# Batch 0's tables on GpSimd's queue, two weight pieces between the thirds of x, and E's rows copied whole

## The chip, the cores and the metric

The kernel runs on one core of one Trainium2 chip. The metric is the device time in microseconds of one execution. Times below are written in us; engines are TensorE (PE in the profile, its weight loads PEld), VectorE (DVE), ScalarE (ACT), GpSimd (POOL) and SyncE (SP), whose queue issues most transfers. Each engine runs its own instructions in the order in which they were issued to it and waits at an instruction until the semaphores that it names have been reached.

## What is computed

```python
X = np.fft.fft(x, axis=1)              # x: (8, 3008, 256) float32
X = np.fft.fft(X, axis=2).real         # Fourier mixing over sequence and features
x = X.reshape(8 * 3008, 256)
gate = 1.0 / (1.0 + np.exp(-(x @ w_gate)))   # w_gate, w_val: (256, 1536) float64
val = x @ w_val
out = gate * val @ w_out                     # w_out: (1536, 256) float64
```

The three weights are given as float64 and are turned into float32 on the chip.

## The kernel before

**The main part.** A batch is mixed in two steps: sums over the sequence with cosine and sine tables give pk and qk (`half`, `places`), and the feature transform is merged into the gate and value weights once, G = dtab x weights (`merge`, line 346, and `merged`, line 353), so that one multiplication of pk and qk with G gives gate and value (`front_a`, line 731, and `front_b`, line 742). The term of the first feature, the row E, is added through ScalarE: `seed` (line 722) writes E's chunk, spread over the partitions in EK, times the vector ge into the accumulator. The loop over `count` steps (8 batches x chunks of 252 positions x 12 tiles of d_ff) then runs front_a, gate_a, part, seed, gate_b, back and front_b, with other work hung on single steps in the dictionaries `mid`, `pre`, `use`, `side`.

**The prologue**, which the change touches, stands before that loop, from `busy = ...` on. Everything is written out by hand in order.

- *Weights* come in 18 pieces of 512 KB: 0 to 11 of gate and value in turn, 12 to 17 of w_out. `weight_load(j)` (line 257) issues the transfer on SP. `weight_parts(j)` (line 303) takes Abs of the high words and a scaled copy of the low words on ScalarE. `weight_join(j)` (line 313) does three VectorE operations through a PSUM bank (lines 322, 323, 325) and an integer add on GpSimd (line 327). `piece(j)` is four matmuls of the joined piece with dt into a bank `ps`; `merged(j)` copies that bank to G on ScalarE (line 358); `ge_load(j)` (line 371) sends two rows of G back through SP as two columns each of ge.
- *x of batch 0* comes in three thirds of 1 MB (`load_third`, line 151, line 155), and its cosine and sine tables in six transfers of 371 KB (`load_table`, line 204, line 206), two for each third. `fold_ops(0, 2)` gives, per third, `third` (lines 498, 499, 460 on VectorE, then a small ScalarE copy of one feature to `XV`, line 516) and `feats` with `turned` (lines 505, 507, 508 on VectorE, line 510 on ScalarE). After `third` and `feats` of a third, `e0_sums(j)` adds its part to row E in bank pe, and `halves` add its part to three of the four halves of pk and qk: (block 0, pk), (block 1, pk), (block 0, qk). Half of these sums read x folded, the other half the turned copies that ScalarE makes. The fourth half, (block 1, qk), runs in one go behind the third third. Each half is then copied (line 578) and placed (lines 584, 588).
- *Row E*: `e0_heads` builds the first 252 values on VectorE (lines 644 to 646), `e0_copies` copies the four rows of bank pe on ScalarE (line 626), `e0_spread` spreads the heads over the partitions with one matmul of one row (ek), and `e0_row` places the whole row on GpSimd at step 4 of the loop.

Transfers use eight semaphores for SP's and ScalarE's queues in turn; a transfer also waits for the one issued eight before it. SP's order is: weights 0 to 3, third 0, two tables, third 1, two tables, third 2, two tables, weights 4 and 5, ge of pieces 0 to 3, weights 6 to 12, and then 14 to 17 with 13 among them, and the rest of ge.

PSUM has eight banks: three (8 - NB) rotate under the tag x, five (NB) have tags of their own, po0 to po4.

Of the kernel before, what the change touches and what calls it, by code (L numbers as in the profile page):

```python
# [53 lines left out]
NQ = 6  # L54
# [28 lines left out]
def kernel(  # L83
# [44 lines left out]
    sp = ctx.enter_context(tc.tile_pool(name="sp", bufs=2))  # L128
    cp = ctx.enter_context(tc.tile_pool(name="cp", bufs=2))
    op = ctx.enter_context(tc.tile_pool(name="op", bufs=1))  # L130
    psx = ctx.enter_context(tc.tile_pool(name="psx", bufs=8 - NB, space=PSUM))
    pso = ctx.enter_context(tc.tile_pool(name="pso", bufs=1, space=PSUM))

    def mm(o, l, r, start, stop):
        nc.tensor.matmul(o, l, r, start=start, stop=stop, skip_group_check=True)  # L135

    def bank(name, other=None):
        if other is not None:
            return pso.tile([P, 512], F32, name=name, tag=f"po{other}")
        return psx.tile([P, 512], F32, name=name, tag="x")  # L140


    X = {}
# [42 lines left out]
    HK = -(-(HE + HO) // 16) * 16  # L186
    n = 2 * NQ * HK
    ST = [st[:, 0:n].rearrange("p (t q k) -> p t q k", t=2, q=NQ)]
    XV = st[0:NP, n : n + 2 * NQ * (HD + 1)].rearrange("p (i q d) -> p i q d", i=2, q=NQ)
    assert NE == HE + HO and NO == 2 * HO and n + 2 * NQ * (HD + 1) <= LONG  # L190
    sgn = const.tile([P, 2], F32, name="sgn")
    wf = const.tile([P, NG, len(PLACE), P], F32, name="wf")
    G = const.tile([P, 2, 2, F], F32, name="G")
# [9 lines left out]

    def load_table(t, j):
        q = slice(2 * j, 2 * j + 2)
        nc.sync.dma_start(out=ST[0][0:NP, t, q, 0 : HE + HO], in_=stab[:, t, q, HO : NE + HO])

    def table_again():

# [225 lines left out]
    def sign(q, r=False):  # L435

        i = (q // 2 % 2) ^ (r and q % 2 == 0)
        return sgn[0:NP, i : i + 1]

    def fold_ops(b, nq):  # L440
# [52 lines left out]
        else:  # L493
# [14 lines left out]
                tt(lo, lo, hi, op=ALU.add)  # L508
            def turned(q):
                copy = lambda to, of, s: nc.scalar.activation(to, of, AF.Copy, scale=s)  # L510
                copy(XV[:, :, q, 0:HD], x4[:, 1::-1, q, 0:HD], sign(q.start))
                for i in range(q.start, q.stop):
                    copy(x4[:, 3:1:-1, i, HD:D], x4[:, 3:1:-1, i, 0:HD], sign(i, True))
            XR_[0] = [(XV[:, i], x4[:, 3 - i, :, HD:D]) for i in range(2)]
            for q in qs:
                ops += [lambda q=q: (third(q), nc.scalar.activation(
                            XV[:, :, q, HD], x4[:, 1::-1, q, HD], AF.Copy, scale=sign(q.start))),
                        lambda q=q: (feats(q), turned(q))]
        for blk, (v, r) in enumerate(parts):
            if b and blk:  # L520
# [8 lines left out]
    def table_of(t, q, blk, turned=False):  # L529

        if not turned:
            return ST[0][0:NP, t, q, blk * HE : HE + blk * HO]
        to = ST[0][0:NP, t ^ (q % 2), q]
        return to[:, HE + HO - 1 : HE - 1 : -1] if blk else to[:, HE - 1 : 0 : -1]

    def columns(blk):

        return (slice(HO, NE), slice(0, HO)) if not blk else (slice(0, HO), slice(HO, NO))

    def half(b, w, d, blk, sn, other=None):  # L540
# [2 lines left out]
        c0, n = ((0, NE), (NE, 2 * NJ if b else NO))[blk]  # L543
        ev, od = [bank(name, other and other[i])[:, 0:n] for i, name in enumerate(("ev", "od"))]

        def sums(*qs):
            for q in sorted(qs, key=lambda q: q % 2):
                mm((ev, od)[q % 2][:, columns(blk)[0]], w(q), table_of(int(sn), q, blk), q < 2, q >= NQ - 2)
            for q in sorted(qs, key=lambda q: q % 2):
                mm((ev, od)[q % 2][:, columns(blk)[1]], XR_[0][blk][int(sn)][:, q, 0:HD],  # L550
                   table_of(int(sn), q, blk, True), False, q >= NQ - 2)

# [29 lines left out]
    def places(d, blk, sn, ev, od, high=None, e=nc.vector):  # L582
        if not high:
            e.tensor_tensor(d[:, blk : blk + 2 * ev.shape[1] - 1 : 2], ev, od, op=ALU.add)
        if high in (None, 1):
            lo, hi = (od, ev) if sn else (ev, od)
            top = M - blk
            e.tensor_tensor(d[:, top : top - 2 * NO + 1 : -2], lo[:, 0:NO], hi[:, 0:NO],
                                    op=ALU.subtract)
# [14 lines left out]

    E0 = {}

    def e0_sums(j):

        if not j:
            E0["ps"] = bank("pe", NB - 1)  # L610
        for q in (2 * j, 2 * j + 1):
            for blk in range(2):
                row = (2 * blk + q % 2) * TB
                mm(E0["ps"][row : row + 1, columns(blk)[0]], W[0, blk][2][:, q], table_of(0, q, blk), not j, j == N3 - 1)
        for q in (2 * j, 2 * j + 1):
            for blk in range(2):
                row = (2 * blk + q % 2) * TB
                mm(E0["ps"][row : row + 1, columns(blk)[1]], XV[:, blk, q, HD : HD + 1],
                   table_of(0, q, blk, True), False, j == N3 - 1)

    def e0_copies():

        ps = E0["ps"]
        E0["v"][3] = evp.tile([P, 2 * NJ], F32, name="a", tag="a")[0:1, 0:NO]
        for i, a in enumerate(E0["v"]):
            nc.scalar.copy(a, ps[i * TB : i * TB + 1, 0 : a.shape[1]])

    def e0_row():

        er = shared["er"]  # L630
        ev, od, ev1, od1 = E0["v"]
        nc.gpsimd.memset(er[:, NK:], 0.0)
        places(er, 0, True, od, ev, e=nc.gpsimd)
        places(er, 1, False, ev1, od1, e=nc.gpsimd)

    def e0_heads():

        n = CH // 2
        full = op.tile([P, NK + 1], F32, name="er", tag="os")
        a = E0["v"] = [full[0:1, i * NE : i * NE + n] for i, n in enumerate((NE, NE, NO))]  # L640
        a.append(evp.tile([P, 2 * NJ], F32, name="a", tag="a")[0:1, 0:NO])
        h = E0["h"] = ekp.tile([P, CH], F32, name="eh", tag="ek")[0:1]
        for i in (1, 2, 3):
            nc.vector.tensor_copy(a[i][:, 0:n], E0["ps"][i * TB : i * TB + 1, 0:n])
        nc.vector.tensor_tensor(h[:, 0::2], a[1][:, 0:n], E0["ps"][0:1, 0:n], op=ALU.add)
        nc.vector.tensor_tensor(h[:, 1::2], a[2][:, 0:n], a[3][:, 0:n], op=ALU.add)

    def e0_spread(other):

        ps = bank("ek", other)[:, 0:CH]  # L650
        mm(ps, busy[0:1, 0:P], E0["h"], True, True)
        EK[0] = ekp.tile([P, CH], F32, name="ek", tag="ek")
        nc.scalar.copy(EK[0], ps)

# [289 lines left out]
    nc.gpsimd.memset(nil, 0.0)  # L944
    nc.scalar.activation(table, nil[:, 0, 0:1], AF.Sigmoid)
    nc.gpsimd.dma_start(out=zero, in_=nil)
    nc.scalar.dma_start(out=dt, in_=dtab.rearrange("(c p) d -> p c d", p=P))
    load_x(0)
    for j in range(4):
        weight_load(j)  # L950
    for j in range(N3):
        load_third(j)
        for t in range(2):
            load_table(t, j)
    for j in (4, 5):
        weight_load(j)

    def warm(n):

        ps = bank("warm", 3)  # L960
        for _ in range(n):
            mm(ps[:, 0:CH], busy[:, 0:P], busy, True, True)
# [3 lines left out]

    shared["er"] = pqp.tile([P, NK + 1], F32, name="er", tag="pk")[0:1]
    signs()
    warm(12)
    for j in range(4):  # L970
        weight_parts(j)
        weight_join(j, j % 3)
        piece(j, (None, None, None, 3)[j])
        if j > 1:
            merged(j - 2)
    merged(2)
    for j in range(3):
        ge_load(j)
    seq_start(0)
    folds = fold_ops(0, 2)  # L980
    halves = [seq_group(0, blk, 0, (2 * blk, 2 * blk + 1)) for blk in range(2)]
    halves.append(seq_group(0, 0, 1))
    for j in range(N3):
        folds[2 * j]()
        e0_sums(j)
        if not j:
            merged(3)
            ge_load(3)
            for i in (6, 7, 8, 9, 10, 11, 12):
                weight_load(i)  # L990
        folds[2 * j + 1]()
        if j == 1:
            weight_parts(4)
        for sums, _, _ in halves:
            sums(2 * j, 2 * j + 1)
    e0_heads()
    weight_join(4)
    halves[0][1]()()
    weight_parts(5)
    weight_join(5)  # L1000
    halves[1][1]()()
    halves[2][1]()()
    halves = [seq_group(0, 1, 1, (0, 1))]
    halves[0][0](*range(NQ))
    weight_parts(6)
    e0_copies()
    weight_join(6, NB - 1)
    weight_parts(7)
    weight_join(7, NB - 1)
    halves[0][1]()()  # L1010
    e0_spread(2)
    weight_parts(8)
    weight_join(8, NB - 1)
    for j in (4, 5, 6):
        piece(j)
    merged(4)
    seed(0)
    weight_parts(9)
    weight_join(9, NB - 1)
    merged(5)  # L1020
    seed(1)
    front_a(0)
    merged(6)
    seed(2)
    piece(7, 1)
    front_a(1)
    weight_parts(10)
    weight_join(10, NB - 1)
    part(0)
    part(1)  # L1030
    for i in (14, 15):
# [17 lines left out]
    def using(j):  # L1049
        weight_use(j, j % 2)  # L1050
        if jobs[j][0] < 2:
            merged(j)
    for j, i in ((11, 1), (12, 3), (13, 5), (14, 6), (15, 8), (16, 10), (17, 12)):
        if j > 10:
            pre.setdefault(i - 1, []).append(lambda j=j: weight_parts(j))
        mid.setdefault(i, []).append(lambda j=j: weight_join(j, 2))
        if jobs[j][0] == 2:
            use.setdefault(i + 2, []).append(lambda j=j: using(j))
# [138 lines left out]
```

## Time and profile before

| | us |
|---|---|
| three runs: median (least, most) | 1924.33 (1923.66, 1926.11) |
| the profiled execution, its own time | 1925.47 |
| its span, first to last instruction | 1923.7 |
| TensorE busy, share of the span | 1912.1, 99% |
| granted TensorE clock | 1.00 |

The span is the stretch that the profile shows; the time of the execution is 1.77 us longer. A timeline row reads: start, duration, engine, line, operation, output<-input, shape, count, and in brackets the idle time before it and what ended it. A float32 matmul leaves two records. Matmul records overlap, so that TensorE's busy share is no measure of its peak; where their starts are spaced evenly the engine is full. The windows view of the first 60 us, busy time of each engine (and number of instructions) in stretches of 10 us:

```profile
core 0: us, PE busy (x) PEld busy (x) DVE busy (x) ACT busy (x) POOL busy (x), PEclk, DMA share, GB/s
0.00:10.00 10.00, 7.93 (x27) 6.49 (x28) 4.75 (x10) 5.19 (x8) 2.74 (x8) 1.00 0.83 292
10.00:20.00 10.00, 8.20 (x48) 5.60 (x47) 9.12 (x17) 3.82 (x8) 4.80 (x3) 1.00 1.06 315
20.00:30.00 10.00, 9.68 (x72) 7.83 (x72) 7.79 (x13) 3.65 (x8) 0.00 (x0) 1.00 0.93 277
30.00:40.00 10.00, 8.81 (x57) 7.98 (x58) 8.04 (x18) 8.13 (x18) 2.60 (x2) 1.00 0.72 256
40.00:50.00 10.00, 10.00 (x46) 8.30 (x45) 9.40 (x16) 9.78 (x21) 4.21 (x4) 1.00 1.02 377
50.00:60.00 10.00, 8.89 (x41) 7.52 (x40) 6.78 (x13) 7.43 (x17) 3.54 (x3) 1.00 0.04 1
```

### The profile page before, as it was taken

The page shows a single profiled execution, that of the slowest core. Times are in us where ns is not written, and L with a number is a line of the kernel's source. Part 1 is how long each engine was busy: PE and PEld are TensorE (multiplying, and loading weights), DVE is VectorE, ACT ScalarE, POOL GpSimd, SP SyncE. Part 2 cuts the span into 40 slices and gives each one's busy share as a digit, 9 for nine tenths or more (in the row PEclk, how much of TensorE's full clock was granted, in tenths as well). Part 3 has the DMA queues.
Part 4 walks back from the last instruction along what each step waited for, and adds up shares of the span by engine and source line. Part 5 has one row for each costly group of instructions (what it writes and reads, how often), then busy time and mean ns, then how long its engine had stood idle before and what let it go on. Part 6 is the DMA issues. An engine that isn't in the chain of part 4 may idle for free.

```text
span 1923.7 us, 34664 instructions
## 1 busy us (share of the span) xinstructions
PE 1912.1 (99%) x11340; PEld 1793.4 (93%) x11340; DVE 1410.9 (73%) x3220; ACT 1346.3 (70%) x3158; POOL 1554.7 (81%) x2807
## 2 busy tenths in 40 slices
PE   8999999999999999999999999999999999999999
PEld 7899999999999999999999999999999999999998
DVE  7757876787767776777777777777777777766776
ACT  5877767767777677776777767777677766777775
POOL 2589989978898688986888878988788886777775
PEclk9999999999999999999999999999999999999999
DMA  9251421111020201202111020111200100000001
GB/s 305 84 91 37 106 80 57 51 62 33 20 77 26 80 18 36 68 15 80 25 48 49 20 81 21 47 51 24 80 14 15 26 16 15 15 22 20 26 17 30
DMA packets 169215, 95.62 MB, mean 50 GB/s; under 512 B 129658, under 2 KB 159940, under 8 KB 167244
## 3 DMA queue, kind: packets, MB, share of 16 engines
q1 hardware_dynamic: 168482, 92.90, 17.0%
q8 instruction: 91, 1.49, 0.3%
q14 instruction: 88, 0.72, 0.1%
q10 hardware_dynamic: 522, 0.50, 0.1%
q0 software_dynamic: 32, 0.00, 0.0%
HBM read 68.13 MB, written 47.24 MB: 60 GB/s over the span
## 4 chain that ended last, share of the span: by engine, by line
PE 96%; ACT 1%; POOL 0%; DVE 0%; issue 0%; ACTq 0%; POOLq 0%
PE pf L135 50%; PE po L135 41%; PE ev L135 2%; PE rows L135 1%; PE od L135 1%; PE row L135 0%; POOL sf L777 0%; ACT pf L729 0%; ACT G L358 0%; ACT ae L740 0%; PE pe L135 0%; ACT wf L311 0%; ACT wc L311 0%; PE ps L135 0%; POOL st L231 0%
## 5 line engine op out<-in xcount | busy, mean ns | idle before, releaser
L777 POOL TENSOR_TENSOR sf<-h 128x168 f32<-128x168 f32 (+1 forms) x935 | 516.7, 571 | 229.8 <-DVE h L771 229.2
L777 POOL TENSOR_TENSOR sf<-h,sf 128x168 f32<-128x168 f32 (+1 forms) x1122 | 614.0, 568 | 49.4 <-DVE h L771 47.9
L135 PE MATMUL pf<-qk,G 128*128 128x252 f32 (+1 forms) x2304 | 582.0, 375 | 1.3 <-ACT ae L740 1.3
L135 PE MATMUL pf<-pk,G 128*128 128x252 f32 (+1 forms) x2304 | 582.5, 376 | 0.0
L729 ACT ACTIVATE pf<-ek,ge 128x252 f32<-128x252 f32 (+1 forms) x1152 | 542.6, 471 | 19.3 <-DVE h L771 0.3
L771 DVE TENSOR_TENSOR h<-pf,z 128x252 f32<-128x252 f32 (+1 forms) x576 | 241.6, 419 | 415.2 <-ACT pf L768 413.6
L135 PE MATMUL po<-sf,wf 128*128 128x168 f32 (+1 forms) x2992 | 516.9, 306 | 0.3 <-POOL sf L777 0.2
L740 ACT ACTIVATE ae<-pf 128x504 f32<-128x504 f32 (+1 forms) x576 | 339.2, 589 | 249.2 <-PE pf L135 248.0
L135 PEld LDWEIGHTS pf<-pk,G 128*128 128x128 f32 x2304 | 437.0, 190 | 51.7 <-issue 2.0
L135 PEld LDWEIGHTS po<-sf,wf 128*128 128x128 f32 x2992 | 460.6, 190 | 9.2 <-POOL sf L777 1.0
L135 PE MATMUL po<-h,wf 128*128 128x168 f32 (+1 forms) x2618 | 463.3, 305 | 0.0
L135 PEld LDWEIGHTS pf<-qk,G 128*128 128x128 f32 x2304 | 410.8, 190 | 27.9 <-ACT ae L740 2.1
L755 DVE TENSOR_TENSOR z<-ae,pf 128x504 f32<-128x504 f32 (+1 forms) x576 | 386.0, 670 | 63.1 <-ACT h L754 58.3
L135 PEld LDWEIGHTS po<-h,wf 128*128 128x128 f32 x2618 | 416.6, 190 | 16.2
L895 DVE TENSOR_TENSOR c<-c 128x168 f32<-128x168 f32 (+1 forms) x929 | 423.5, 464 | 3.4
L754 ACT ACTIVATE h<-pf 128x252 f32<-128x252 f32 (+1 forms) x576 | 218.5, 379 | 208.5 <-PE pf L135 199.8
L767 DVE TENSOR_TENSOR h<-h,pf 128x252 f32<-128x252 f32 (+1 forms) x576 | 233.5, 405 | 0.0
L768 ACT ACTIVATE pf<-z 128x252 f32<-128x252 f32 (+1 forms) x576 | 211.4, 367 | 23.4 <-DVE h L767 20.1
L777 POOL TENSOR_TENSOR sf<-sf 128x168 f32<-128x168 f32 (+1 forms) x187 | 104.2, 557 | 14.7
L777 POOL TENSOR_TENSOR sf<-sf,h 128x168 f32<-128x168 f32 (+1 forms) x187 | 110.3, 590 | 0.0
L808 ACT COPY c<-po 128x504 f32<-128x504 f32 (+1 forms) x141 | 80.0, 568 | 0.0
L904 DVE STREAM_TRANSPOSE os<-c 128x256 f32<-128x256 f32 x184 | 79.9, 435 | 0.0
(168 smaller groups left out, 921.9 us busy)
## 6 DMA issues: line engine op xcount, KB each, us to landing
x<-xr SPq DMA_DIRECT2D x14, 1536.0 KB
out_dram<-os SPq DMA_DIRECT2D x368, 56.0 KB
xr<-in_xf_dram SPq DMA_DIRECT2D x14, 768.0 KB
xr<-in_xf_dram SPq DMA_DIRECT2D x35, 256.0 KB
ek<-ed SPq DMA_DIRECT2D x39, 126.0 KB
out_dram<-os SPq DMA_DIRECT2D x284, 7.0 KB
x<-in_xf_dram SPq DMA_DIRECT2D x3, 1024.0 KB
st<-in_stab_dram SPq DMA_DIRECT2D x4, 564.8 KB
```

The lines of the kernel that those rows point to most:

```text
L135: nc.tensor.matmul(o, l, r, start=start, stop=stop, skip_group_check=True)
L729: nc.scalar.activation(PF[i][:, g], EK[i // NFT], AF.Copy, scale=ge[:, g, f : f + 1])
L740: nc.scalar.activation(AP[i], PF[i], AF.Copy, scale=2.0)
L754: nc.scalar.activation(H[p][:, fh, 0:n], PF[i][:, 0], AF.Sigmoid)
L755: nc.vector.tensor_tensor(z[:, :, ::-1], AP.pop(i), PF[i], op=ALU.subtract)
L767: nc.vector.tensor_tensor(h[:, fh, 0:n], h[:, fh, 0:n], pf[:, 1], op=ALU.mult)
L768: nc.scalar.activation(pf[:, 0], z[:, 0], AF.Sigmoid)
L771: nc.vector.tensor_tensor(h[:, fh, n:], pf[:, 0], z[:, 1], op=ALU.mult)
L777: nc.gpsimd.tensor_tensor(block(p, dst), block(p, a), block(p, b), op=(ALU.subtract, ALU.add)[op])
L808: (nc.vector.tensor_copy if t == 1 or t == 3 and not last else nc.scalar.copy)(C[0][:, 3 * t * R : 3 * (t + 1) * R], PO[t][:, 0 : 3 * R])
L895: engine.tensor_tensor(t[:, dst * R : (dst + 1) * R], *v, op=(ALU.subtract, ALU.add)[op])
L904: nc.vector.transpose(os_[0][:, s, 0:nb, h, :], t[:, c0 : c0 + nb * TB])
```

## The change

1. **Queues.** dt moves from ScalarE's queue to SP's, behind weights 0 and 1. The six table transfers move from SP to GpSimd: the first two behind a one-element copy that waits for dt and ahead of the adds of joins 0 to 3, the other four behind those adds. SP issues weights 0, 1, dt, weights 2, 3, the three thirds, weights 4 to 7, then ge of pieces 0 to 3, weights 8 to 12.
2. **Order of ScalarE.** `merged` of pieces 0 to 2 comes after all four pairs of parts.
3. **Pieces 4 and 5.** Piece 4's parts follow third 0's turned rows on ScalarE, its join comes on VectorE between thirds 1 and 2, its matmuls between the sums of thirds 1 and 2; piece 5's parts follow third 1's turned rows, its join comes behind third 2. Joins 6 to 10 and the banks of all joins and pieces are set anew. Within a third, the sums that read x folded come before those that read turned rows. Join 11 moves from step 1 of the loop to step 2.
4. **Row E.** One ScalarE copy takes all of bank pe (128 x 377); four transfers on SP bring its four rows to partition 0; the spread is two matmuls of 126 columns with a 0/1 matrix `pair`, built with four memsets on GpSimd. Bank pe is cleared by a VectorE memset first. `e0_heads` and the three other copies go. The one turned feature lies in a tile of its own, `xe`.
5. The three rotating banks get tags x0 to x2, which the prologue can name.

```diff
-        nc.sync.dma_start(out=ST[0][0:NP, t, q, 0 : HE + HO], in_=stab[:, t, q, HO : NE + HO])
+        nc.gpsimd.dma_start(out=ST[0][0:NP, t, q, 0 : HE + HO], in_=stab[:, t, q, HO : NE + HO])
...
     def e0_copies():
-        ps = E0["ps"]
-        E0["v"][3] = evp.tile([P, 2 * NJ], F32, name="a", tag="a")[0:1, 0:NO]
-        for i, a in enumerate(E0["v"]):
-            nc.scalar.copy(a, ps[i * TB : i * TB + 1, 0 : a.shape[1]])
+        t = E0["v"] = evp.tile([P, 2 * NJ], F32, name="a", tag="a")[:, 0:NE]
+        nc.scalar.copy(t, E0["ps"][:, 0:NE])
+        full = op.tile([P, NK + 1], F32, name="er", tag="os")[0:1]
+        for i, n in enumerate((NE, NO)):
+            E0[i] = [full[:, (2 * i + r) * NE - i * r : (2 * i + r) * NE - i * r + n] for r in range(2)]
+            for r, to in enumerate(E0[i]):
+                row = (2 * i + r) * TB
+                nc.sync.dma_start(out=to, in_=t[row : row + 1, 0:n])
...
     def e0_spread(other):
         ps = bank("ek", other)[:, 0:CH]
-        mm(ps, busy[0:1, 0:P], E0["h"], True, True)
+        for i in range(2):
+            mm(ps[:, i::2], pair[:, i], E0["v"][:, 0 : CH // 2], not i, True)
...
-    nc.scalar.dma_start(out=dt, in_=dtab.rearrange("(c p) d -> p c d", p=P))
     load_x(0)
     for j in range(4):
         weight_load(j)
+        if j == 1:
+            nc.sync.dma_start(out=dt, in_=dtab.rearrange("(c p) d -> p c d", p=P))
     for j in range(N3):
         load_third(j)
-        for t in range(2):
-            load_table(t, j)
-    for j in (4, 5):
+    for j in (4, 5, 6, 7):
         weight_load(j)
...
     signs()
+    for i in range(2):
+        for h in range(2):
+            nc.gpsimd.memset(pair[h * HP : (h + 1) * HP, i], float(i == h))
+    E0["ps"] = bank("pe", NB - 1)
+    nc.vector.memset(E0["ps"][:, 0:NE], 0.0)
     warm(12)
+    nc.gpsimd.tensor_copy(xe[0:1, 0, 0:1], dt[0:1, 0, 0:1])
+    for t in range(2):
+        load_table(t, 0)
     for j in range(4):
         weight_parts(j)
         weight_join(j, j % 3)
-        piece(j, (None, None, None, 3)[j])
-        if j > 1:
-            merged(j - 2)
-    merged(2)
+        piece(j, ("x0", "x1", "x2", 3)[j])
+    for j in (1, 2):
+        for t in range(2):
+            load_table(t, j)
+    for j in range(3):
+        merged(j)
...
     for j in range(N3):
+        qs = (2 * j, 2 * j + 1)
         folds[2 * j]()
-        e0_sums(j)
         if not j:
+            e0_sums(j)
             merged(3)
             ge_load(3)
-            for i in (6, 7, 8, 9, 10, 11, 12):
+            for i in (8, 9, 10, 11, 12):
                 weight_load(i)
+        else:
+            e0_sums(j, (0,))
+        if j == N3 - 1:
+            merged(4)
         folds[2 * j + 1]()
-        if j == 1:
+        for sums, _, _ in halves[0:2]:
+            sums(*qs, which=(0,))
+        if j:
+            e0_sums(j, (1,))
+        for sums, _, _ in halves[0:2]:
+            sums(*qs, which=(1,))
+        halves[2][0](*qs)
+        if j == 0:
             weight_parts(4)
-        for sums, _, _ in halves:
-            sums(2 * j, 2 * j + 1)
-    e0_heads()
-    weight_join(4)
+        elif j == 1:
+            weight_join(4, "x2")
+            piece(4, "x2")
+            weight_parts(5)
+    weight_join(5, "x2")
     halves[0][1]()()
-    weight_parts(5)
-    weight_join(5)
     halves[1][1]()()
+    weight_parts(6)
     halves[2][1]()()
+    weight_join(6, 2)
+    e0_copies()
+    weight_parts(7)
     halves = [seq_group(0, 1, 1, (0, 1))]
     halves[0][0](*range(NQ))
-    weight_parts(6)
-    e0_copies()
-    weight_join(6, NB - 1)
-    weight_parts(7)
-    weight_join(7, NB - 1)
+    weight_join(7, 3)
     halves[0][1]()()
-    e0_spread(2)
     weight_parts(8)
-    weight_join(8, NB - 1)
-    for j in (4, 5, 6):
-        piece(j)
-    merged(4)
+    e0_spread(NB - 1)
+    weight_join(8, 2)
+    turns["x"] = 2
+    piece(5, "x0")
     seed(0)
+    front_a(0)
+    merged(5)
     weight_parts(9)
-    weight_join(9, NB - 1)
-    merged(5)
+    weight_join(9, 3)
     seed(1)
-    front_a(0)
+    piece(6, "x1")
+    piece(7, 1)
+    front_a(1)
     merged(6)
     seed(2)
-    piece(7, 1)
-    front_a(1)
...
-    for j, i in ((11, 1), (12, 3), (13, 5), (14, 6), (15, 8), (16, 10), (17, 12)):
+    for j, i in ((11, 2), (12, 3), (13, 5), (14, 6), (15, 8), (16, 10), (17, 12)):
```

## The prediction

> **What bounds the kernel now.** I read the page's busy shares and its 40 slices first, then the chain of waits, then the timeline of the first 66 us.
>
> ```profile
> PE 1912.1 (99%) x11340; PEld 1793.4 (93%) x11340; DVE 1410.9 (73%) x3220; ACT 1346.3 (70%) x3158; POOL 1554.7 (81%) x2807
> PE   8999999999999999999999999999999999999999
> POOL 2589989978898688986888878988788886777775
> ```
>
> TensorE is full in every slice but the first (48 us each). What can be won or lost lies in the prologue.
>
> ```profile
> 59.67 0.49 ACT ae L740
> 60.16 0.04 issue
> 60.20 1.99 PE pf L135 x8
> 62.20 1.73 PE ps L135 x8
> ```
>
> In the chain of waits (start, us, what) every piece from 60.20 on is TensorE; before it the chain goes through ACT and VectorE. From 60.20 to the end (1923.7) TensorE never waits again for long, and the change leaves that work alone. So the kernel's time moves by as much as this point moves. The timeline says how it comes about:
>
> ```profile
> 1.34 0.79 POOL L946 DMA_DIRECT2D zero<-nil  x1 [0.30 <-POOL nil L944]
> 12.55 0.69 DVE L322 TENSOR_SCALAR join<-wqk 128x512 f32<-128x512 f32 x1 [0.59 <-ACT wqk L309]
> 14.83 2.23 POOL L327 TENSOR_TENSOR wqk<-wqk,raw 128x512 int32<-128x512 int32 x1 [1.44 <-ACT G L358]
> 15.96 2.38 DVE L460 TENSOR_TENSOR x<-x 126x512 f32<-126x512 f32 x2
> 25.11 0.17 DVE L498 TENSOR_TENSOR x<-x 126x4 f32<-126x4 f32 x1 [1.23 <-DMA x<-in_xf_dram]
> 29.68 0.66 ACT L309 ACTIVATE wqk<-raw 128x512 f32<-128x512 f32 x1 [3.06 <-DMA raw<-in_moe_w_gate_dram]
> 31.12 0.50 PE L135 MATMUL pe<-st 126*1 126x188 f32 x8 [1.36 <-ACT st L516]
> 31.74 0.59 DVE L644 COPY er<-pe 1x126 f32<-1x126 f32 x2 [2.43 <-PE pe L135]
> 39.73 0.69 PE L135 MATMUL ek<-eh,busy 1*128 1x252 f32 x2
> ```
>
> Two more rows price the loads: the issues of the tables on SP (ns, least/median/most), and the DMA view of the first 31 us, 0.775 us a number.
>
> ```profile
> L206 SPq DMA_DIRECT2D st<-in_stab_dram x6: 380/1056/3584, 3.9 to 15.2; - x6
> ```
>
> ```profile
> GB/s 0 0 48 174 357 385 411 399 407 410 407 410 410 407 396 312 230 240 226 259 373 410 382 263 291 296 244 275 359 396 334 246 253 290 284 336 336 135 33 6
> ```
>
> The last third of x lands at 25.1 us (VectorE waited 1.23 us for it), weight piece 4 at 29.7 us (ACT waited 3.06 us, and the third's turned sums behind it). From 31.74 to 51.86 us (end of piece 10's join) VectorE has seven joins and the sums' placing with hardly a gap: 19.2 busy of 20.2 us.
>
> **The change, part by part.**
>
> *Start.* The four copies of G leave the gaps between ACT's weight parts. That removes VectorE's 0.59 us before join 3. dt goes from ACT's queue to SP's, third in order: the same bytes ahead of x, so what x sees is nothing; weight 0 may land up to 0.6 us earlier (256 KB at the 408 GB/s of the busiest stretch), but the third of x that VectorE needs next is behind all of it. GpSimd gets four small memsets and a one-element copy that waits for dt (about 7.0 us: weight 1 with dt beside it, as many bytes, landed at 6.97), and behind that copy stand two table loads and the four adds of the joins. A table load on GpSimd is not in this trace. Nearest rows: 0.79 us for zero<-nil, two rows, on GpSimd itself; 0.38 to 3.58 us for the same tables on SP, waits included. I take 1 us, by the first row, which is on the right engine, and keep 3.6 for the range. Two loads end at 9; join 0's add, at 7.98 before, starts then; the third add ends by 12.9, before join 3's at 14. Hidden. The first third of x shares the DMA engines with its tables from some 9 us on, where before it went ahead of them; it needed to be there at 14.63. Its flow would end at 11.2 (3.41 MB, by the GB/s row); sharing makes it 13.4, and about 1 us to landing gives 14.4. So I book the 0.59 us as eaten: third 0 starts at 14.6 as before, bounds -0.6 and +1.6 (if the tables go first). Thirds 0 and 1 then end at 23.9 as before.
>
> *Piece 4 between the thirds.* SP now issues x alone and then weights 4 to 7, GpSimd issues tables 1 and 2 after join 3's add, at 17.1. Two kinds of bytes decide when weight 4 lands. At 17.8 us, where the row drops to 263, the second third had flowed before, and would now. Left are third 2 and weight 4, 1.57 MB = 3.85 us alone at 408 GB/s, and 6.4 us of tables (3.1 to 3.2 us a pair: the row shows the first one as its four numbers from 230 to 259, from 12.4 to 15.5 us). Tables flow from about 18.7; sharing evenly from there the weights' flow ends at 17.8 + 0.9 + 2 x 2.95 = 24.6, and with the 1.2 us to landing that 25.1 and 29.7 show, weight 4 lands at **25.8**, not 29.7. Bounds: 22.9 (no table goes beside it) and 29.7 (all do). Tables 1 land at some 26 us instead of before 24; TensorE's third 1 waits for them and for ACT's turned rows, which are queued behind piece 4's parts (28.9), and ends by 31.0, piece 4 by 32.7. That is covered because VectorE's third 2 comes later still:
>
> VectorE: Abs on ACT to 26.5; join 4, three operations of 0.69 and gaps, to 28.6; third 2 and its features took 25.11 to 29.31, 4.20 us; and join 4's add on GpSimd now runs beside them. The trace prices that: the same pair at 14.83 and 15.96, where the add took 2.23 instead of 1.29 us and one L460 1.65 instead of 0.69, cost VectorE 0.96. So third 2 is ready at 33.8 instead of 29.3. The Trainium skill (SBUF — State Buffer, "Who interferes with whom") has the rule for it: a VectorE operation with two SBUF inputs blocks against a GpSimd instruction that reads SBUF until the first is through; by it the price would be up to the whole add, 1.29, and the end 0.3 us later. The trace agrees in kind.
>
> TensorE: sums of third 2, 0.75 + 24 passes x 0.16 = 4.6, then the fourth half 3.84: done at 42.2, against 39.73. It is 2.5 us late and has done one piece more (8 passes x 0.216 = 1.73).
>
> *After that.* Work from 39.73 to 60.20 was 56 ps passes x 0.216 + 28 pf x 0.2125 + ek 0.43 = 18.5 of 20.5 us. Less piece 4: 16.8. So 42.2 + 16.8 = 59.0, 1.2 us earlier, if TensorE never waits. VectorE: the 20.1 us from 31.74 to 51.86 lose E's heads (31.74 to 33.15, 1.41) and join 4 (2.1): 16.6, so 33.8 + 16.6 = 50.4, 1.5 earlier. ACT: 31.75 to 49.52, 17.8 us, loses three of the four 0.47 us copies of E's rows (1.40), piece 5's parts (1.25) and piece 4's copy (0.57): 33.85 + 14.55 = 48.4, 1.1 earlier. Join 11 one step later takes its 2.05 us (54.41 to 56.46 in the chain) away from between two z. All three queues come out 1.1 to 1.5 us ahead; TensorE's bound has no idle in it where there were 1.95 us. I take 0.3 of idle: **-0.9 us**.
>
> *The rest, at nothing:* four 1.5 KB row copies on SP, about 0.47 us each, wait for ACT near 39 us and hold back the last five weight loads by some 4 us; the first of those was loaded at 39.88 and is read at 67.93. E's rows (POOL at 64.14) wait for these copies, landed by some 46. The spread is two matmuls of 126 columns where one of 252 was. The eight ge rows of pieces 0 to 3, now behind weights 4 to 7, are read at 43.18; the loads behind them started at 31.50 and would at some 32.
>
> **Sum.** Span 1923.7 - 0.9 = 1922.8. The profiled execution took 1925.47, 1.77 around the span and 1.14 above the median of the three runs; against that median: 1924.33 - 0.9 = **1923.4**.
>
> **Rivals.**
>
> *The tables stay out of the ring's way (better).* Weight 4 at 22.9, join 4 straight after third 1 (24.0 to 26.1), no blocking: third 2 ready at 30.3, fourth half at 38.7, plus 16.8 = 55.5; with 0 to 2 us of idle 2.7 to 4.7 earlier, say 3.7: 1920.6. For it: with tables alone 226 to 259 GB/s pass, with weights 408, so filling in may help. Against: the same view has the engines nine tenths busy in both stretches. The Trainium skill (DMA: Bandwidth & Descriptors, "Issuing engines are not separate DMA queues") says that transfers of all issuing engines interleave on the same 16 engines and only issue time is saved; by it this case is out, and no row here shows two loaded queues.
>
> *Table loads are dear on GpSimd (slower).* Six loads of P us, five adds and piece 4's matmuls stand in one line: third 2's sums can't start on TensorE before 7 + 6P + 5 x 1.29 + 1.7 = 15.2 + 6P. That passes 33.8 at P = 3.1. At 4 us it is 39.2, 5.4 later: +4.5, **1928.8**. For it: each load has 252 rows, the 0.79 us had two; that one took 5.4 us to land. Against: the small one is near a fixed cost. The Trainium skill (SBUF — State Buffer, "SBUF: two separate sides") warns that GpSimd can't write descriptors while VectorE runs its fast two-port mode; that would be a P of this size. The joins' operation (L322) takes 0.69 us for 512 elements, no quicker per element than L499's 1.21 for 1020, so the trace shows no fast mode there.
>
> *The change does not free weight 4.* If the tables pass in front (29.7), ACT, which has parts 4 ahead of third 1's turned rows, and VectorE wait 3.9 us longer: +3.0, 1927.3; halfway, 1925.3.
>
> **How the numbers follow.** Forecast 0.48 (its own range 1921.6 to 1925.0), better 0.19, dear loads 0.17, weight 4 late 0.16. A measurement of this kernel can tell 0.2%, 3.85 us, from no change: below 1920.5 or above 1928.2. Of the better case about half (0.10) and of the forecast's tail 0.05 lie below: 0.15. Of the dear loads most (0.14), and of the late weight 0.03, lie above: 0.17. The rest, 0.68, can't be told from no change. The range 1920.0 to 1927.8 leaves out the dear loads and the best of the better case.
>
> **What would show it.** POOL's table rows near 1 us (3 or more: the second rival). ACT's wait before piece 4's Abs ending near 25.8. L507 (before: L499) or L468 beside join 4's add stretched by about 1 us. Third 2's first e0 sums at 33.8 and the chain's first long run of TensorE at 59.3. Wrong if that run starts before 56.5 or after 62, or if TensorE waits again behind it.

## The result and the profile after

| | before | after |
|---|---|---|
| median of the compared runs, us (least to most; 16 each) | 1924.66 (1923.62 to 1926.82) | 1928.28 (1925.93 to 1930.31) |
| the profiled execution: time / span, us | 1925.47 / 1923.7 | 1927.97 / 1926.2 |
| point from which TensorE never waits, us | 60.20 | 62.53 |

The ratio is 1.0016, 95% interval 1.0009 to 1.0023: a small loss, but clear of the scatter. By the two medians the changed kernel is 3.6 us slower. The two profiled executions differ by 2.5 us, 2.3 of them at that point; before's lay 0.8 above its median, after's 0.3 below. The forecast was 0.9 us faster, and the time lies 0.5 us above the forecast's range.

The page after, busy shares and TensorE's slices: as before, full in every slice but the first.

```profile
PE 1913.5 (99%) x11342; PEld 1795.6 (93%) x11342; DVE 1411.9 (73%) x3216; ACT 1345.4 (70%) x3155; POOL 1561.1 (81%) x2818
PE   8999999999999999999999999999999999999999
```

The chain of waits after (start, us, what):

```profile
5.67 22.40 DMA raw<-in_moe_w_gate_dram
...
29.49 0.62 ACT st L518
...
30.16 0.76 PE ev L135 x2
30.92 0.63 PE od L135 x2
...
34.02 0.32 PE ev L135 x2
...
62.53 1.99 PE pf L135 x8
```

Near its head stands one piece of 22.4 us that before's chain doesn't have: the transfer of weight 4, counted from its issue, so that most of it is its turn in SP's queue behind the three thirds of x. Behind it come ScalarE's turned rows and then TensorE. The timeline after, rows of several engines (L506, L507 and L468 are before's 498, 499 and 460; L317, L330 and L335 its 309, 322 and 327):

```profile
6.87 1.62 POOL L214 DMA_DIRECT2D st<-in_stab_dram  x2
13.75 0.17 DVE L506 TENSOR_TENSOR x<-x 126x4 f32<-126x4 f32 x1
28.09 0.66 ACT L317 ACTIVATE wqk<-raw 128x512 f32<-128x512 f32 x1 [7.62 <-DMA raw<-in_moe_w_gate_dram]
28.78 0.69 DVE L330 TENSOR_SCALAR join<-wqk 128x512 f32<-128x512 f32 x1 [5.75 <-ACT wqk L317]
29.55 0.50 PE L135 MATMUL pe<-st,xe 126*1 126x188 f32 x8 [4.11 <-ACT xe L524]
31.07 2.21 POOL L335 TENSOR_TENSOR wqk<-wqk,raw 128x512 int32<-128x512 int32 x1 [11.88 <-DVE wqk L333]
32.17 2.39 DVE L468 TENSOR_TENSOR x<-x 126x512 f32<-126x512 f32 x2
45.13 0.61 PE L135 MATMUL ek<-a,pair 128*128 128x126 f32 x4
```

Three engines wait for one transfer. ScalarE has piece 4's parts ahead of third 1's turned rows, and TensorE waits 4.11 us for those; VectorE has join 4 ahead of third 2 and waits 5.75 us. Third 0 starts 0.9 us earlier than before (13.75 against 14.63), and that is lost here. The fourth half ends, and E's spread (ek) begins, at 45.13 instead of 39.73.

The transfers by queue in the changed kernel, from 21 to 25 us (packets, MB, share of the 16 engines' time; q0 is GpSimd's queue with the tables, q1 SP's with x and the weights):

```profile
q0 software_dynamic: 200, 0.70, 65.1%
q1 hardware_dynamic: 205, 0.40, 38.2%
```

As many packets of each, but the tables' are 3.5 KB and SP's 1.95 KB: SP gets 0.10 MB per us. From 25 to 28 us it is 144 packets with 0.48 MB against 143 with 0.28. From 18 to 21 us, when the tables had hardly begun, the same view reads:

```profile
q1 hardware_dynamic: 493, 0.98, 89.8%
q0 software_dynamic: 47, 0.16, 15.9%
```

From 21 to 25 us, 65.1% of 16 engines over 4 us makes 208 ns for each of the tables' packets, and 38.2% makes 119 ns for each of SP's; from 18 to 21 us one of SP's took 87 ns.

### The profile page after: what moved, and what is told of

It reads as the page before. It is cut to its first block, busy times and chain, and to the rows that moved or that the text cites. A ratio compares the mean times of both kernels' runs of the same rounds, so it can differ in the third digit from the quotient of the medians.

```text
span 1926.2 us, 34679 instructions
## 1 busy us (share of the span) xinstructions
PE 1913.5 (99%) x11342; PEld 1795.6 (93%) x11342; DVE 1411.9 (73%) x3216; ACT 1345.4 (70%) x3155; POOL 1561.1 (81%) x2818
## 4 chain that ended last, share of the span: by engine, by line
PE 96%; POOL 2%; DMA 1%; ACT 0%; SPq 0%; issue 0%; DVE 0%; ACTq 0%; POOLq 0%
PE pf L135 50%; PE po L135 40%; PE ev L135 3%; DMA raw<-in_moe_w_gate_dram 1%; POOL sf L773 1%; PE rows L135 1%; PE od L135 1%; PE ps L135 0%; PE row L135 0%; POOL x L485 0%; PE pe L135 0%; POOL x L463 0%; POOL x L465 0%; POOL st L235 0%; SPq L161 0%
```

## The experiments

T1: weight 4's transfer, since pieces 4 and 5 stand between the thirds, sets the end. T2: the halved TensorE clock behind the 4 us wait costs. T3: GpSimd's queue slows the transfers, and that is the loss wherever the pieces stand. T4: row E's new form costs. Ratios are against the kernel before in the same session (its medians 1924.5 to 1925.0).

**1. Tables back on SP, pieces still between the thirds.**

```diff
     for j in range(N3):
         load_third(j)
+        for t in range(2):
+            load_table(t, j)
...
-        nc.gpsimd.dma_start(out=ST[0][0:NP, t, q, 0 : HE + HO], in_=stab[:, t, q, HO : NE + HO])
+        nc.sync.dma_start(out=ST[0][0:NP, t, q, 0 : HE + HO], in_=stab[:, t, q, HO : NE + HO])
...
```

The issues of the tables among GpSimd's instructions go, and so does the one-element copy ahead of them.

> The changed kernel, but the six table transfers are issued by SP again in the order of before (third 0, its two tables, third 1, its two, third 2, its two, then weight 4); pieces 4 and 5 stay between the thirds, row E stays as changed. Theory T1 (piece 4's transfer, standing between TensorE's thirds, sets the end): weight 4 lands where it did before, near 29.7 instead of 28.1, so everything behind join 4 is about 1.6 us later and the time is 1929 to 1930.5, above the changed kernel's 1928.3. Rival T3 (GpSimd's queue slows the transfers and is what costs): the time falls to 1925 to 1926.5. Rival T4 (row E's new form costs): as the changed kernel, 1928.

Measured: 1931.28 (ratio 1.0035, 1.0023 to 1.0047). ScalarE took weight 4 at 30.89, TensorE waited 6.86 us. T1 held, though weight 4 came 1.2 us later than it said and the time is 0.8 us above its range; T3 as the whole cause fell.

**2. The queues alone, on the kernel before.** Its order of pieces, row E and ScalarE; tables on GpSimd, dt and weights 6, 7 moved up on SP.

> The kernel before with part 1 of the change alone: the tables on GpSimd's queue, dt, x and weights 0 to 7 on SP's; pieces 4 and 5 behind the thirds, row E by its old form. T1: nothing waits for weight 4 between the thirds, third 0 is some 0.9 us earlier, and TensorE's order is that of before; the time is 1923.5 to 1924.7, no later than before's. T3: the slower transfers show here alone, 1926 to 1928.

Measured: 1927.81 (1.0016, 1.0007 to 1.0025): T3's number, a miss for T1 as told. But x was not slower, VectorE began third 2 at 24.63 without a wait (25.11 before). The timeline of this run:

```profile
13.38 0.69 DVE L322 TENSOR_SCALAR join<-wqk 128x512 f32<-128x512 f32 x1 [1.45 <-ACT wqk L309]
27.66 0.49 PE L135 MATMUL pe<-st 126*1 126x188 f32 x4 [1.72 <-DMA st<-in_stab_dram]
```

GpSimd issues two tables ahead of join 0's add, which moves to 8.79 (7.98 before); piece 0 and its `merged`, which stands ahead of weight 3's parts on ScalarE, follow, and third 0 starts at 15.46. Tables 1 then land at 27.6, later than TensorE wants them. Part 1 costs by itself where nothing else is changed with it.

**3. Pieces 4 and 5 behind the thirds**, queues and row E as changed.

```diff
-        if j == N3 - 1:
-            merged(4)
         folds[2 * j + 1]()
+        if j == 1:
+            weight_parts(4)
...
-        if j == 0:
-            weight_parts(4)
-        elif j == 1:
-            weight_join(4, "x2")
-            piece(4, "x2")
-            weight_parts(5)
-    weight_join(5, "x2")
+    weight_join(4, "x2")
     halves[0][1]()()
+    weight_parts(5)
+    weight_join(5, "x2")
...
+    piece(4, "x2")
     piece(5, "x0")
+    merged(4)
```

> The changed kernel with pieces 4 and 5 taken out from between the thirds: piece 4's parts follow third 1's turned rows on ScalarE, join 4 follows third 2's features on VectorE, pieces 4 and 5 follow the spread of E's row on TensorE. Queues and row E stay as changed. T1: TensorE's wait of 4.1 us between the sums of third 1 is gone; third 2's features follow its landing near 24 to 25 and end near 29, the fourth half ends at 37 to 38 instead of 45.1, and the time is 1921.5 to 1924, below the changed kernel by 4 us or more. T3 and T4 (queue or row E at fault): 1927 or more, as what they blame is still in it.

Measured: 1923.18 (0.9993, 0.9984 to 1.0002), 5.1 us below the changed kernel. Its timeline:

```profile
26.25 0.17 DVE L506 TENSOR_TENSOR x<-x 126x4 f32<-126x4 f32 x1 [2.82 <-DMA x<-in_xf_dram]
38.88 0.61 PE L135 MATMUL ek<-a,pair 128*128 128x126 f32 x4
```

VectorE waits for x alone, and the fourth half ends 6.2 us earlier than in the changed kernel, with piece 4 still to do (1.7 us). T1 held in the time; third 2 landed later than its 24 to 25 us, and the fourth half ended at 38.88, not at 37 to 38.

**4. Weight 4 issued ahead of third 2**, nothing else.

> The changed kernel with one transfer moved: weight 4 is issued ahead of third 2 of x, nothing else. T1: weight 4 lands some 2.5 us earlier (near 25 to 25.5) and third 2 some 1.3 to 2 us later, which nobody reads until join 4 is through; TensorE's wait shrinks from 4.1 to 1 to 1.5 us and the time falls by 2 to 3 us, to 1925 to 1926.5. T3 and T4: no change, 1928.

Measured: 1924.06 (1.0001, 0.9992 to 1.0010): 0.9 us better than expected. ScalarE took weight 4 at 21.00 without a wait. Third 2 then landed at 28.05; VectorE waited 2.67 us for it, and TensorE only 0.73:

```profile
28.05 0.17 DVE L506 TENSOR_TENSOR x<-x 126x4 f32<-126x4 f32 x1 [2.67 <-DMA x<-in_xf_dram]
32.30 0.59 PE L135 MATMUL ev<-st,x 126*128 126x189 f32 x2 [0.73 <-DVE x L516]
```

One transfer moved takes off 4.2 us of the median. Two of the eleven executions took 1928.3 and 1929.2 us all the same; why is not shown.

**5. Row E alone, on the kernel before.**

> The kernel before with part 4 of the change alone (bank pe cleared first, one copy of it, four transfers for E's rows, spread by two matmuls with pair); queues, order and pieces as before, and without the separate tile for the turned feature. T1 (weight 4's place and landing make the loss): VectorE loses the 1.4 us of heads, TensorE was waiting for its joins at 40 to 46, so 1923 to 1925. T4 (row E costs): 1926 or more.

Measured: 1925.23 (1.0002, 0.9993 to 1.0011): no difference to before, T4 fell.

**6. Run 2 with `merged` of pieces 0 to 2 behind all parts.**

> The kernel of the second run (queues alone on the kernel before, 1927.8) with one more part of the change: merged of pieces 0 to 2 behind all four pairs of parts on ScalarE. Its profile showed two losses: VectorE waited 1.45 us for weight 3's parts behind merged of piece 0, so that third 0 began at 15.5 instead of 14.6, and TensorE waited 1.72 us for tables 1. If both are real, this order gives back the first alone: third 0 begins near 13.8, the wait for tables 1 stays or grows to 2 to 3 us, and the time falls by 0 to 1 us, to 1926.8 to 1927.8. Rival (the ScalarE order is all of it): 1924 to 1925. Rival (GpSimd's queue slows x itself): third 1 or 2 is what TensorE waits for.

Measured: 1926.29 (1.0008, 0.9999 to 1.0017), 1.5 us less than run 2. Third 0 started at 13.76, and TensorE still waited 1.38 us for tables 1, where 1.72 or more was expected. So the loss by ScalarE's order was real, and the time fell 0.5 us further than expected; what the wait for the tables costs was not tried by itself. Another 3.1 us lie between run 6 and run 3. VectorE stood 4.04 us before E's heads (L644) in run 6, which run 3 doesn't have; the other edits between the two were not told apart.

**7. Seven extra matmuls in TensorE's wait.**

```diff
+        if j == 1:
+            warm(7, "x2")
         if j:
             e0_sums(j, (1,))
```

> The changed kernel with seven extra matmuls (results unused, bank x2) on TensorE between the sums of third 1 that read x folded and those that read turned rows, so that TensorE isn't idle for 4 us there. T2 (the half clock after that wait is what costs): the pairs that took 0.63 us each take 0.32, and the 1.9 us come off the end: 1926.4. T1: the sums of third 1 end 1.9 us earlier but then wait for join 4 and for third 2's features (ready at 36.0 against 36.3 at which they were used), so at most 0.4 us: 1927.8 to 1928.3.

Measured: 1929.01 (1.0023, 1.0015 to 1.0032), no gain, but it decides nothing: in the profiled execution weight 4 came at 29.98, a wait of 3.16 us stayed behind the seven, and the turned sums of third 1 ran at half the clock, so that third 2's sums began 1.4 us after their features were ready (39.34 against 37.90).

**8. Run 3 with the tables of third 2 issued by SP behind third 2.**

```diff
...
     for j in range(N3):
         load_third(j)
+    for t in range(2):
+        load_table(t, 2, nc.sync)
...
```

> The third run's kernel (pieces 4 and 5 behind the thirds, 1923.2) with the tables of third 2 issued by SP behind third 2 of x and ahead of weight 4, instead of by GpSimd beside them. In that run third 2 landed at 26.25 with these tables beside it, and TensorE had no wait over 0.2 us behind 32. T1: 0.74 MB less goes beside third 2, so it lands 1.5 to 2.5 us earlier, and with it everything to the end: 1921 to 1922. Rival (the rate is set by the tables' small rows wherever they go, or VectorE's joins bind next): 1923.

Measured: 1923.96 (0.9994, 0.9985 to 1.0002), no gain, and yet third 2 landed by 23.1. The timeline of ScalarE:

```profile
30.93 0.66 ACT L317 ACTIVATE wqk<-raw 128x512 f32<-128x512 f32 x1 [6.10 <-DMA raw<-in_moe_w_gate_dram]
```

Weight 4, now behind these tables, is waited for once more (4.89 us in run 3): its parts stand ahead of third 2's turned rows, and TensorE waited 0.88 us for those. It is the changed kernel's mistake in small. Nor could the early landing help at once: TensorE was at third 1's sums until 29.5.

**9. The changed kernel with the tables of third 2 issued by SP behind weight 4.**

> The changed kernel with the tables of third 2 issued by SP behind weight 4 instead of by GpSimd beside it; pieces 4 and 5 stay between the thirds. This gives weight 4 the landing that the prediction had for it, 25.8, without moving it in SP's order. T1: ScalarE takes weight 4 near 25.5 to 26.5 instead of 28.09, third 2's features end near 34, and the time falls by 2 to 3 us, to 1925 to 1926.5 (the prediction's sum for that landing was 1923.4 to 1924.5). Rival (the landing isn't what sets the end, but the half clock or VectorE's row of work): 1927.5 or more.

Measured: 1926.37 (1.0006, 0.9998 to 1.0015), 1.9 us less than the changed kernel, though weight 4 came at 27.41 only (the tables of third 1 still go beside it). T1 held in the time, the landing was a miss. (The profiled execution was the slowest of the eleven, 1927.08.)

**10. Piece 4's parts behind third 1's turned rows on ScalarE.**

> The changed kernel with piece 4's parts behind third 1's turned rows on ScalarE instead of ahead of them; join 4 stays ahead of third 2 on VectorE. It takes ScalarE's part of the wait away and leaves VectorE's. T1 as first told (TensorE's 4.1 us wait for the turned rows is the loss): the wait goes and the time falls by 2 us or more, to 1926. T1b (VectorE's wait for join 4 ahead of third 2 is what sets the end): TensorE only waits later, 4 to 5 us for join 4 and third 2, and the time stays at 1927.5 to 1929.

Measured: 1929.52 (1.0020, 1.0011 to 1.0029). The wait moved: TensorE finished third 1 at 28.7 and then stood 6.39 us before piece 4. The time is 0.5 us above T1b's range, and weight 4 came later in this profile (29.90) than in that of the changed kernel (28.09). T1b: VectorE's order, join 4 ahead of third 2, carries the loss. No gain from ScalarE's order by itself shows.

**11. Run 8 with piece 4's parts behind third 2's turned rows.**

> The eighth run's kernel (pieces behind the thirds, tables of third 2 by SP, 1924.0) with piece 4's parts behind third 2's turned rows on ScalarE. In the eighth run third 2 was ready on VectorE 2.5 us earlier than in the third, but ScalarE stood 6.10 us at weight 4, which landed at 30.93, ahead of third 2's turned rows, and TensorE waited. T1: third 2's sums follow its features at 27.2 at once, the fourth half ends near 34 instead of 36.6 to 39.5, and TensorE may then wait for join 4 (weight 4 near 30.9): 1922 to 1923.3. Rival (VectorE's joins behind bind): 1924, no change.

Measured: 1923.21 (0.9991, 0.9982 to 0.9999). ScalarE's wait of 6.10 us is gone, but in this execution third 2 landed at 25.42 (23.1 in run 8), and its sums began at 29.73, no earlier than in run 8 (29.54). The fourth half ended at 38.54, not near 34: the time lies in T1's range, but not by T1's way. Against run 8 it is 0.75 us less, and the intervals of the two overlap.

**12. Weight 4 ahead of third 2, its tables by SP behind it, piece 5's parts last.**

```diff
...
     for j in range(N3):
+        if j == N3 - 1:
+            weight_load(4)
         load_third(j)
-    for j in (4, 5, 6, 7):
+    for t in range(2):
+        load_table(t, 2, nc.sync)
+    for j in (5, 6, 7):
...
             piece(4, "x2")
-            weight_parts(5)
+    weight_parts(5)
     weight_join(5, "x2")
```

> The changed kernel with weight 4 issued ahead of third 2 (as in the fourth run), the tables of third 2 issued by SP behind third 2, and piece 5's parts behind third 2's turned rows on ScalarE; piece 4 stays between the thirds. T1: weight 4 lands near 21 to 22, third 2 near 25.5 instead of 28.05, its features end near 29.7, TensorE has piece 4 to do up to 31.1 and then goes on without a wait; the fourth half ends near 39.3 with piece 4 done, which is 1.8 us ahead of the third run: 1920.5 to 1922.5. Rival (tables 1 or the joins behind bind instead): 1923.5 or more.

Measured: 1922.88 (0.9991, 0.9982 to 1.0000), 0.4 us above T1's range and 0.6 below the rival's. Weight 4 was there when ScalarE came to it (20.91); third 2 landed at 26.80, not 25.5, and the fourth half ended at 40.22, not 39.3.

**13. The tables of GpSimd's queue cut in two.**

```diff
-        q = slice(2 * j, 2 * j + 2)
-        nc.gpsimd.dma_start(out=ST[0][0:NP, t, q, 0 : HE + HO], in_=stab[:, t, q, HO : NE + HO])
+        for q in (2 * j, 2 * j + 1):
+            nc.gpsimd.dma_start(out=ST[0][0:NP, t, q, 0 : HE + HO], in_=stab[:, t, q, HO : NE + HO])
```

> The changed kernel with each table transfer on GpSimd cut in two (one q each, 126 rows, 186 KB), so twelve issues instead of six. In the profile of the changed kernel GpSimd's queue and SP's move as many packets each while both are loaded (200 and 205 from 21 to 25 us), of 3.5 and 1.95 KB. Theory P (the engines take a packet of each queue in turn): if the cut makes GpSimd's packets smaller, SP's share rises with the ratio of sizes, to some 0.15 to 0.2 MB per us beside the tables; if their size stays, so does the share of 0.10. Rival (a share by time, or GpSimd's queue ahead): 0.10 MB per us whatever the size. The time: with smaller packets weight 4 lands nearer 26 but the tables of thirds 1 and 2 later (six more issues of 0.77 us), so 1926 to 1929.

Measured: 1930.47 (1.0026, 1.0016 to 1.0036); weight 4 came at 30.64. The queues of this run from 21 to 25 us:

```profile
q0 software_dynamic: 238, 0.68, 64.5%
q1 hardware_dynamic: 233, 0.44, 41.7%
```

As many packets of each again. Those of the tables shrank from 3.5 to 2.9 KB only, so the test was a weak one; the ratio of bytes went from 1.75 to 1.55, that of the packets' sizes from 1.79 to 1.51. That goes with theory P; the 0.15 MB per us expected of smaller packets was a miss (0.11), and so was the time, 1.5 us above the range.

**14. Extra matmuls through the whole wait**, in free columns of bank pe.

```diff
...
+        if j == 1:
+            for _ in range(22):
+                mm(E0["ps"][:, 384:510], busy[:, 0:P], busy[:, 0:126], False, True)
```

> The changed kernel with 22 short extra matmuls (126 columns, results unused, in columns of bank pe that nothing reads) on TensorE between the sums of third 1 that read x folded and those that read turned rows, about 4.8 us, so that TensorE works up to some 30 us. T2 (the half clock after that wait costs): 1 to 1.9 us less than the changed kernel, 1926.5 to 1927.3. T1: third 2's features, ready near 36 with weight 4's landing, are what TensorE then waits for: at most 0.4 us less, 1927.9 to 1928.5.

Measured: 1927.95 (1.0016, 1.0008 to 1.0025), 0.3 less than the changed kernel and not to be told from it. The clock stayed at full speed in the profiled execution. Run 9 is the match to it: there weight 4 came at nearly the same time (27.41 against 27.29), the clock fell to 0.55 from 30 to 33 us (1.00 here), and yet third 2's sums began at 35.54 against 35.35 and both spans are 1925.3. T2 as the main cause fell.

**15. Run 12 with 15 opening matmuls instead of 12.**

> The twelfth run's kernel (weight 4 ahead of third 2, its tables by SP behind it, piece 5's parts last; 1922.9) with 15 instead of 12 of the unused matmuls that open TensorE's work. In the twelfth run TensorE stood 2.04 us between these and piece 0 and then ran at 0.58 of its clock from 12 to 15 us, so that piece 3 ended 0.8 to 1.7 us later than in runs without that gap. Theory: the gap falls below 1.4 us, the clock stays up, third 0's sums begin near 18.1, and the time falls by 0.3 to 0.8 us, to 1922 to 1922.6. Rival (the landing of tables 1 and third 2 sets the end anyway): no change, 1922.9.

Measured: 1922.64 (0.9990, 0.9982 to 0.9999), the fastest of all. TensorE's gap before piece 0 fell from 2.04 to 0.49 us and its clock in the next 3 us rose from 0.58 to 1.00; against run 12 the 0.24 us can't be told from nothing. (The profiled execution was the slowest of the eleven, 1924.21.) What TensorE still waits for in this run:

```profile
27.56 0.49 PE L135 MATMUL pe<-st,xe 126*1 126x188 f32 x4 [1.48 <-DMA st<-in_stab_dram]
```

These are the tables of third 1, on GpSimd's queue.

**Weight 4 against the end.** All profiles in which weight 4 was waited for with join 4 ahead of third 2:

| run | ScalarE takes weight 4, us | span, us |
|---|---|---|
| 14 | 27.29 | 1925.3 |
| 9 | 27.41 | 1925.3 |
| after | 28.09 | 1926.2 |
| 10 | 29.90 | 1928.6 |
| 7 | 29.98 | 1929.2 |
| 13 | 30.64 | 1928.9 |
| 1 | 30.89 | 1928.7 |

The end moves by about 1 us for each us of this landing. Runs 7, 10 and 14 have the transfers of the changed kernel unaltered; in them and in the changed kernel's own profile weight 4 came between 27.29 and 29.98. Only one execution of each kernel was profiled; that this scatter is what spreads the changed kernel's times over 4.4 us (before's over 3.2) is likely, but not shown. Run 12's eleven spread over 1.8 us.

## Why the prediction was wrong

- *The bound* (the end moves with the point from which TensorE never waits): held. That point moved by 2.33 us, the span by 2.5. At 62.53 it lies past the 62 that the prediction named as a sign of being wrong.
- *Start:* held, on the good side. Tables took 0.77 us each to issue on GpSimd (booked 1), landing 9.2 us later. VectorE's 0.59 us went, and third 0 was there in time: 13.75, where 14.6 was booked. The dear-loads rival is out.
- *Weight 4 at 25.8:* **this step failed.** It shared the DMA engines evenly between x and weights on SP and the tables on GpSimd, half of 408 GB/s for SP, 0.20 MB per us. The trace shows packets taken in turn, the tables' nearly twice as long, and 0.10 MB per us. The turn is nearly the whole of it: one packet of each takes 208 + 119 = 327 ns, in which 16 engines move 16 x 1.95 KB for SP, 0.095 MB per us; with SP's 87 ns it would be 0.106. Why SP's packets took longer beside the tables is not shown. The Trainium skill (DMA: Bandwidth & Descriptors, "Queues, rings and completion order") states the rule: an engine goes round the queues that have work and takes a whole packet of each. The trace agrees (200 packets against 205; 238 against 233 in run 13). So weight 4 came at 28.09 in the profiled execution and up to 29.98 with the same transfers in others, though the tables began to flow only at about 20 us, not at 18.7. Run 9, with the tables of third 2 out of its way, and run 4, with the transfer moved ahead, take back 1.9 and 4.2 us.
- *Third 2 ready at 33.8:* the working held, 2.2 us later. Join 4's add and VectorE's pair took 2.21 and 2.39 us beside each other, where they take 1.29 and 1.42 apart: VectorE lost 0.97 us, and 0.96 was booked.
- *The fourth half done at 42.2:* it was done at 45.13. Of the 2.9 us between, 2.2 are weight 4's; 0.3 is the wait for piece 4 behind the half clock; third 2's sums took 5.0 instead of 4.6.
- *After that 16.8 + 0.3 of idle:* 17.4; an ordinary miss of 0.3. Row E's new form alone cost nothing that shows (run 5).
- *The rivals:* weight 4 late is what happened. It was priced at 1925.3 for 27.75 and 1927.3 for 29.7; the median, 1928.28, is above both, and its chance was given as 0.16. The better case, weight 4 at 22.9 beside the tables, came in no run. With the transfer moved ahead (run 4) it was there by 21.00, but third 2 then came at 28.05, and the time was 1924.06, not 1920.6.
- *The baseline:* between the forecast and the median lie 4.9 us. The spans account for 3.4 of them (1926.2 against 1922.8). The rest is the chance of single executions: before's profile lay 1.14 us above the median that the forecast was laid on, after's 0.3 below its own.

What the forecast missed in judgement: it saw that ScalarE's and VectorE's orders made piece 4 a gate for thirds 1 and 2, and booked that as covered by a landing time that it had only estimated. Without the gate (run 3) the kernel stands 1.3 us below the kernel before of its session, just not told from it; with the gate it stands 3.6 above.

## What to carry to other kernels

Work put into a gap waits for its data with everything queued behind it on each in-order engine, so before moving a step forward look for its transfer's place in the queue, and move the transfer first. A transfer on a second queue is not free filling: count packets and their time, not bytes, to see what is left for the first queue. Keep what gates little (tables of the last third, a later weight) behind what gates much, in the same queue, where their order is yours to set (run 12).

## What the runs showed of the hardware

- Two loaded queues shared the DMA engines by packets, one for one: 200 against 205 in the changed kernel, 196 against 198 in run 4 and 238 against 233 in run 13, all from 21 to 25 us. In the changed kernel SP's 0.38 of the engines' time moved 0.40 MB in 4 us; from 18 to 21 us, nearly alone, its queue moved 0.98 MB in 3 us with 0.90 of it.
- TensorE's matmuls took twice as long behind waits of 3.2 to 6.9 us: a pair of the sums every 0.63 us instead of 0.32, for 3.7 us in the changed kernel. The Trainium skill (TensorE: Matmul & The Clock Gate, "Part 1: The HAM clock gate") gives an idle window of about 3.4 us for it. Here waits of 1.91 to 2.04 us before piece 0 (runs 4, 6, 10, 12) were already followed by clocks of 0.55 to 0.58 from 12 to 15 us, while one of 1.77 us there (run 13) was not, and neither was one of 2.34 us before piece 3 in run 2 (1.00 from 15 to 20 us). So the length of the wait alone doesn't decide it. On the kernel's time the half clock behind the 4 us wait cost little, since third 2 was waited for anyway (run 14).
